# Spectral and token mixer on one core: the spectral path moved back by one pair, and VectorE and ScalarE held to the written order in the second product

## The chip, the core and the metric

One core of a Trainium2 chip runs the whole program in one launch. TensorE multiplies matrices into PSUM, VectorE and ScalarE do the elementwise work, GpSimd and SyncE issue most of the transfers. The metric is device time in microseconds (us), and lower is better. The kernel before took 385.02 us, the median of three runs (384.89 to 386.52).

## What is computed

The input `x` has 2048 tokens of 512 channels, all in float32. The reference is

```
xn = layernorm(x)
s  = irfft2( rfft2(xn) * (w_r + 1j*w_i) )            # over tokens and channels
h  = layernorm(xn)
u  = gelu( einsum("bsd,sf->bdf", h, w1) + b1 )       # F = 1792, along the tokens
y  = einsum("bdf,fs->bds", u, w2) + b2
out = x + s * silu(y transposed back)
```

The change lies in the last third of the kernel: the product with `w2`, the gate `silu(y)`, the last transforms of the spectral path (`s`), and `x + s * gate`.

## The kernel before, in words

**The second product.** The 2048 output tokens form 16 row blocks of 128 tokens (`NJ`), taken as eight pairs: block `p` and block `p + 8`. A pair is a 2 x 2 block product by Strassen's scheme in Winograd's form, so seven products of half size stand in place of eight. They run in the order `ORDER = (1, 2, 5, 6, 3, 7, 4)`, and this text calls them product 1, product 2, product 5 and so on. Each is 21 matmuls: seven blocks along F, and for each the three terms high x high, high x low and low x high of a split of float32 into two parts (`FORMS`, line 140 in the profile, since the helper that records TensorE's work has that line).

**PSUM in a pair.** Products 1, 6, 7 and 4 add up in bank `bx`, product 2 goes to `by`, and products 5 and 3 add up in `bz`. Between them the running sums are read out: `p1` copies `bx` after product 1, `p5` copies `bz` after product 5, `v2` copies `bx` after product 6 (`copied`, line 883, ScalarE). `summed` (line 891, VectorE) adds a bank and such a copy: `c11 = by + p1`, `c12 = bz + v2`, `c22 = bx + p5`. `gate` (line 887, ScalarE) is the Silu of that. So product 6 must not write `bx` before `p1` is read, nor product 3 write `bz` before `p5` is, nor product 7 `bx` before `v2`, nor product 4 before `c22`.

**Weights of a product ("forms").** Each product needs its own combination of blocks of `w2`, split in two: ScalarE writes the high part (line 749, here "high 5" for product 5), VectorE the low part (line 750, "low 5"). The forms lie in three buffers (`w2p`, tag `w2f`, `bufs=3`), so the form of a product can be written once the product three places before it has ended. Products 5, 6 and 3 take theirs from one tile, `s1`, that is changed in between: low 5, then `s1 += a12`, high 6, low 6, `s1 += a11`, high 3, low 3 (`added_up`, line 759, VectorE, "add"). The blocks come by DMA one pair ahead (line 736 on SyncE, and line 738 on GpSimd, which adds a second block on top of the first).

**The spectral path of a pair.** `gathered` (lines 831 to 836) collects the pair's frequencies in `yt`, with one small ScalarE copy and two VectorE operations for each block. `channels` (TensorE, into banks 6 and 7) is the inverse transform along the channels; the profile shows it as `ps<-cd,yt`. `unfolded` (lines 851 to 867) turns that into `y` in three pieces: a ScalarE copy with a sum and a difference; four sums; two scaled sums. `spectral` (`ps<-y,cft`, banks 0 and 1) is the last transform along the tokens. `finish` (lines 895 to 902) multiplies it by the gate and sends the block out, which GpSimd's transfer adds to `x` in the output; the last block adds `x` on VectorE.

**What sets the order.** The framework orders each engine's instructions by its own model, unless an instruction is kept in program order: then it stands behind all that was recorded for its engine before it. `Kept` wraps an engine so that each of its operations is kept. In the kernel before, TensorE is kept from the middle of the kernel on, VectorE and ScalarE are kept by `step` for the stretch ahead of the loop over pairs (`in_order`), and free in the loop itself. Each engine works off its instructions one after another.

**The start of the loop.** Ahead of it the last blocks of the hidden layer are made: `gelu`, and the parts of `u` in the combinations that the products read. `form_d` serves product 1, `form_a` products 2 and 3, `form_c` products 5 and 6, `form_b` products 7 and 4 (high part line 312, low part line 313, `sums` lines 338 to 341 between `form_a` and `form_c`). Block 6 of `u` is the last, and the last that each product reads. In the kernel before, the order at this place was: forms d, c and b of block 5, form of product 5, then a, sums, c, `s1 += a12` and b of block 6. `gathered(0)` came next, and `channels(0)` stood behind product 2 of pair 0. Later pairs have `spectral(p)` and `channels(p+1)` between products 7 and 4 of pair `p`.

Of the kernel before, what the change touches and what calls it, by code (L numbers as in the profile page):

```python
# [142 lines left out]
def spectral_mixer_kernel(tc, x, w1, b1, w2, b2, wk, we, wx, c_f, c_ft, c_d, c_i, c_g, c_h, c_t, out):  # L143
# [14 lines left out]
    with tc.tile_pool(name="ps", bufs=1, space=PSUM) as psp, ExitStack() as left, ExitStack() as right:  # L158
# [141 lines left out]
        def step(instruction):  # L300
            return keep(instruction) if in_order else instruction
# [439 lines left out]
        def s1_load(p, where):  # L741
            return w2_load("s1", where, p + NP, 0, (p + NP, 1))

        def w2_form(name, src):
# [4 lines left out]
            step(A.activation(parts[:, 0], v, AF.Copy))  # L749
            step(V.tensor_sub(parts[:, 1], v, parts[:, 0].bitcast(F32)))  # L750
            return wf

        nxt = {"a12": w2_load("a12", w2p, 0, 1, queue=G), "a11": w2_load("a11", w2p, 0, 0, queue=G)}
        in_order.append(True)
# [3 lines left out]
        def added_up(t, other):  # L758
            step(V.tensor_add(t, t, other))  # L759

        def w2_forms():

            for p in range(NP):
                yield w2_form(f"1_{p}", cur["a12"])
                yield w2_form(f"2_{p}", cur["a11"])
                yield w2_form(f"5_{p}", cur["s1"])
                if p:
                    added_up(cur["s1"], cur["a12"])
                w = w2_form(f"6_{p}", cur["s1"])
                if p + 1 < NP:  # L770
                    nxt["s1"] = s1_load(p + 1, (w2p, fp)[(p + 1) % 2])
                    nxt["a12"] = w2_load("a12", w2p, p + 1, 1)
                yield w
                added_up(cur["s1"], cur["a11"])
# [12 lines left out]
                yield w  # L787
# [18 lines left out]
        form_a(6)  # L806
        sums(6)
# [5 lines left out]
        lstage.close()  # L813
        fp = pool(left, "left", "fin", 1)
        cur["a21"] = w2_load("a21", fp, NP, 0)
        T = Kept(nc.tensor, keep)
        halved = (slice(0, 64), slice(0, None, 2)), (slice(64, P), slice(1, None, 2))
        xr = fp.tile([P, D], F32, name="xr")
        for rows, tokens in halved:
            SY.dma_start(xr[rows], x[tokens, NJ - 1])  # L820

        def gathered(p):

# [23 lines left out]
        def unfolded(p):  # L847

            pe = ps[:, 6:8].rearrange("p i (h k) -> p i h k", h=2)
            od = fp.tile([P, 2, 256], F32, name=f"od{p}", tag="od")  # L850
            A.activation(od, pe[:, :, 1], AF.Copy)
            es = fp.tile([P, 2, 2, 2, P], F32, name=f"es{p}", tag="es")
            V.tensor_add(es[:, :, 0].rearrange("p i b c -> p i (b c)"), pe[:, :, 0], od)  # L853
            V.tensor_sub(es[:, :, 1].rearrange("p i b c -> p i (b c)"), pe[:, :, 0], od)  # L854
            yield
            t = od.rearrange("p a b -> p (a b)")[:, :256].rearrange("p (i h c) -> p i h c", i=2, h=2)
            V.tensor_add(t[:, :, 0], es[:, :, 1, 1, :64], es[:, :, 1, 1, 64:])
            V.tensor_sub(t[:, :, 1], es[:, :, 1, 1, 64:], es[:, :, 1, 1, :64])
            y = fp.tile([P, 2, 2, 2, 2, 64], F32, name=f"y{p}", tag="y")
            ev = es[:, :, :, 0].rearrange("p i h (q c) -> p i h q c", c=64)  # L860
            ov = es[:, :, 0, 1].rearrange("p i (h c) -> p i h c", c=64)
            V.tensor_add(y[:, 0, :, :, 0], ev[:, :, :, 0], ov)  # L862
            V.tensor_sub(y[:, 1, :, :, 0], ev[:, :, :, 0], ov)  # L863
            yield
            ev = ev[:, :, :, 1].rearrange("p i h c -> p (i h) c")
            for s, sc in ((0, RT), (1, -RT)):
                V.scalar_tensor_tensor(y[:, s].rearrange("p i h q c -> p (i h) q c")[:, :, 1], t.rearrange("p i h c -> p (i h) c"), sc, ev, op0=ALU.mult,
                                       op1=ALU.add)
            ys[p] = y.rearrange("p s i h q c -> p s i (h q c)")
            yield  # L870
# [30 lines left out]
                else:  # L901
                    SY.dma_start(out[tokens, j, cols], g[rows, cols])

        left_, right_, whole = slice(0, HD), slice(HD, D), slice(0, D)
        yts, ys, pieces, gathering = {}, {}, iter(()), iter(())
        run(gathered(0))
        for p in range(NP):
            j0, j1 = p, p + NP
            more = p + 1 < NP
            g0, g1 = (fp.tile([P, D], F32, name=f"g{j}", tag="g", bufs=2) for j in (j0, j1))  # L910
            bx, by, bz = ps[:, 2 + p % 2, :HD], ps[:, 4, :HD], ps[:, 5, :HD]
            for k, n in enumerate(ORDER):
                wf = ready.pop(0)
                w = next(wforms, None) if p + k else None
                if w is not None:
                    ready.append(w)
                o = {1: bx, 6: bx, 7: bx, 4: bx, 2: by, 5: bz, 3: bz}[n]
                for m, i in enumerate(FORMS):
                    uh, ul = form_parts(n, i)
                    for a, (wi, ui) in enumerate(((0, uh), (0, ul), (1, uh))):  # L920
                        T.matmul(o, wf[:, wi, i], ui, start=m + a == 0 and n in (1, 2, 5), stop=m == NH - 1 and a == 2,
                                 skip_group_check=n in (6, 3, 7, 4))
                if n == 1:
                    p1 = copied(f"p1_{p}", bx)
                    if more and p:
                        gathering = gathered(p + 1)
                elif n == 5:
                    p5 = copied(f"p5_{p}", bz)
                    if more and not p:
                        gathering = gathered(p + 1)  # L930
                elif n == 2:
                    gate(g0, j0, left_, summed(f"c11_{p}", by, p1), 1.0)
                    if p == 0:
                        channels(p)
                        pieces = unfolded(p)
                elif n == 6:
                    v2 = copied(f"v2_{p}", bx)
                    if not more:
                        spectral(p)
                elif n == 3:  # L940
                    gate(g0, j0, right_, summed(f"c12_{p}", bz, v2), 1.0)
                    if not more:
                        finish(g0, j0, whole)
                elif n == 7:
                    gate(g1, j1, right_, summed(f"c22_{p}", bx, p5), -1.0)
                    if more:
                        spectral(p)
                        run(gathering)
                        channels(p + 1)
                        pieces = unfolded(p + 1)  # L950
                        finish(g0, j0, whole)
                    else:
                        finish(g1, j1, right_)
                else:
                    gate(g1, j1, left_, bx, -1.0)
                    finish(g1, j1, whole if more else left_)
                if n in (2, 5, 6, 3, 1, 4):
                    next(pieces, None)
                    if n != 4:
                        next(gathering, None)  # L960


# [35 lines left out]
```

## Time and profile before

| | |
|---|---|
| median of 3 runs | 385.02 us |
| profiled execution, its own time | 384.9 us |
| its span in the profile | 382.9 us |
| outside the span | 2.0 us |
| granted TensorE clock, mean | 0.993 |
| VectorE busy, 232.4 to 355.6 us (six pairs) | 101.0 of 123.2 us |
| ScalarE busy, the same stretch | 62.7 of 123.2 us |

A row of the timeline gives the start in us from the start of the span, the duration, the engine, the line, the operation with its tiles and shapes, and how many instructions were merged; brackets give the engine's idle time ahead of it and what ended it. `PE` is TensorE, `DVE` VectorE, `ACT` ScalarE. A row of the stretches gives, for a window of time, each engine's busy time with its instruction count, then the granted clock of TensorE, the DMA share and GB/s. TensorE's ends are modelled, so starts are used here, and a product is measured from its start to the next product's.

### The profile page before, as it was taken

Reading aid. Unit: us, or ns where it says so; the run is one execution under the profiler, and the core shown is the slowest. Engines: PE = TensorE matmul, PEld = TensorE weight load, DVE = VectorE, ACT = ScalarE, POOL = GpSimd, SP = SyncE. Lnnn points to the kernel's source line nnn. Section 1 sums busy time; section 2 is a strip of 40 time slices with the busy share of each in tenths; the row PEclk is TensorE's granted clock in tenths of the full one; section 3 lists DMA queues with packets and bytes.
Section 4 is the critical chain, followed back from the end, with each engine's and each line's share of the span. In section 5 each row is a group of like instructions: output and inputs, shape, how many; then the busy total and the mean of one; then the engine's idle time right before and its main releaser. Section 6 shows DMA issues by size and latency. Waiting matters only on the chain.

```text
span 382.9 us, 7730 instructions
## 1 busy us (share of the span) xinstructions
PE 370.4 (97%) x2888; PEld 321.1 (84%) x2888; DVE 322.4 (84%) x643; ACT 211.1 (55%) x382; POOL 86.2 (23%) x139
## 2 busy tenths in 40 slices
PE   8999999999999999999999599999999999999993
PEld 4888888888878777777888599999999989898993
DVE  6899999984689999999998989788787879796762
ACT  4676776762963444476547644645554553636341
POOL 1133223231222222221020014040313122140301
PEclk9999999999999999999999899999999999999998
DMA  7884776304375565866465598696969687885703
GB/s 238 289 283 165 261 256 243 98 1 125 103 237 205 184 229 183 265 199 215 142 242 96 171 225 156 184 195 161 201 154 239 127 234 139 230 148 160 104 0 55
DMA packets 34404, 68.35 MB, mean 178 GB/s; under 512 B 4656, under 2 KB 17856, under 8 KB 34240
## 3 DMA queue, kind: packets, MB, share of 16 engines
q1 hardware_dynamic: 25920, 43.09, 34.9%
q0 software_dynamic: 8448, 24.78, 29.2%
q8 instruction: 22, 0.36, 0.4%
q14 instruction: 14, 0.11, 0.1%
HBM read 59.47 MB, written 8.13 MB: 177 GB/s over the span
## 4 chain that ended last, share of the span: by engine, by line
PE 86%; DVE 9%; ACT 3%; issue 1%; POOL 0%; ACTq 0%; POOLq 0%
PE ps L140 61%; PE ps L408 20%; PE ps L247 4%; DVE w2f L750 3%; DVE s L759 2%; ACT w2f L749 2%; PE ps L397 1%; DVE yt L836 1%; DVE yt L835 1%; DVE g L895 1%; DVE es L854 0%; DVE es L853 0%; DVE c L891 0%; DVE y L862 0%; DVE y L863 0%
## 5 line engine op out<-in xcount | busy, mean ns | idle before, releaser
L408 PE MATMUL ps<-h,w1h 128*128 128x512 f32 x224 | 58.5, 398 | 0.0
L140 PE MATMUL ps<-h,w1h 128*128 128x512 f32 x176 | 56.2, 400 | 0.0
L408 PEld LDWEIGHTS ps<-h,w1h 128*128 128x128 f32 x224 | 40.9, 188 | 7.9
L750 DVE TENSOR_TENSOR w2f<-s,w2f 128x896 fp32r<-128x896 f32 x32 | 34.9, 1091 | 11.9 <-ACT w2f L749 11.0
L140 PE MATMUL ps<-fa,w2f 128*128 128x256 f32 x336 | 43.6, 281 | 1.1 <-DVE w2f L750 1.1
L140 PEld LDWEIGHTS ps<-fa,w2f 128*128 128x128 f32 x336 | 40.7, 188 | 3.0 <-DVE w2f L750 2.2
L140 PE MATMUL ps<-fb,w2f 128*128 128x256 f32 x336 | 42.5, 280 | 0.6 <-DVE c L891 0.6
L749 ACT ACTIVATE w2f<-s 128x896 fp32r<-128x896 f32 x32 | 32.8, 1026 | 15.5 <-DVE s L759 15.5
L140 PE MATMUL ps<-fc,w2f 128*128 128x256 f32 x336 | 41.2, 282 | 0.0
L140 PEld LDWEIGHTS ps<-fb,w2f 128*128 128x128 f32 x336 | 40.3, 188 | 0.8 <-issue 0.8
L140 PEld LDWEIGHTS ps<-h,w1h 128*128 128x128 f32 x176 | 31.6, 188 | 10.7 <-issue 4.9
L140 PEld LDWEIGHTS ps<-fc,w2f 128*128 128x128 f32 x336 | 40.4, 191 | 0.0
L738 POOL DMA_DIRECT2D s<-in_w_dram x16 | 14.0, 883 | 106.2 <-DMA s<-in_w_dram 60.1
L750 DVE TENSOR_TENSOR w2f<-a,w2f 128x896 fp32r<-128x896 f32 x24 | 26.1, 1092 | 11.3 <-ACT w2f L749 10.6
L140 PE MATMUL ps<-h,w1l 128*128 128x512 f32 x88 | 34.4, 391 | 0.0
L749 ACT ACTIVATE w2f<-a 128x896 fp32r<-128x896 f32 x24 | 24.8, 1038 | 16.8 <-PE ps L140 9.1
L900 POOL DMA_DIRECT2D out_dram<-g x30 | 25.2, 983 | 36.7 <-DVE g L895 30.7
L408 PE MATMUL ps<-h,w1l 128*128 128x512 f32 x112 | 30.6, 389 | 0.0
L408 PEld LDWEIGHTS ps<-h,w1l 128*128 128x128 f32 x112 | 21.0, 188 | 4.5
L591 POOL DMA_DIRECT2D xc<-xc x16 | 9.8, 620 | 64.1 <-ACT xc L588 46.6
L140 PEld LDWEIGHTS ps<-cd,yt 128*128 128x128 f32 x128 | 15.7, 200 | 10.1 <-issue 5.7
L403 DVE TENSOR_TENSOR w1l<-w1r,w1h 128x512 fp32r<-128x512 f32 (+1 forms) x32 | 20.9, 652 | 2.1 <-ACT w1h L400 1.9
(114 smaller groups left out, 700.4 us busy)
## 6 DMA issues: line engine op xcount, KB each, us to landing
a<-in_w_dram SPq DMA_DIRECT2D x22, 448.0 KB, 4.0
wt<-in_wk_dram POOLq DMA_DIRECT2D x16, 512.0 KB, 5.3
s<-in_w_dram SPq DMA_DIRECT2D x16, 448.0 KB, 4.2
s<-in_w_dram POOLq DMA_DIRECT2D x16, 448.0 KB, 6.3
w1s<-in_w_dram SPq DMA_DIRECT2D x36, 128.0 KB, 2.6
w1r<-in_w_dram SPq DMA_DIRECT2D x16, 256.0 KB, 3.1
xc<-xc POOLq DMA_DIRECT2D x16, 256.0 KB, 3.0
x<-in_x_dram SPq DMA_DIRECT2D x15, 256.0 KB, 3.8
```

The source lines that it names most:

```text
L140: return lambda *args, **kw: self.keep(operation(*args, **kw))
L247: T.matmul(z[:, b], h[:, b * P:(b + 1) * P], c, start=True, stop=True)
L397: T.matmul(ps[:, 0], wz[:, :P], wz, start=True, stop=True)
L403: keep(V.tensor_sub(dst, src, hi.bitcast(F32)))
L408: T.matmul(ps[:, bank + i], w[wi][:, i * P:(i + 1) * P], hj, start=first and j == 0, stop=last and j == NJ - 1)
L591: keep(G.dma_start(*(v.rearrange("p s t c -> p s (t c)") for v in (there[c::2], here[1 - c::2, ::-1]))))
L738: G.dma_start(t, w2_half(*added), accum_op=ALU.add)
L749: step(A.activation(parts[:, 0], v, AF.Copy))
L750: step(V.tensor_sub(parts[:, 1], v, parts[:, 0].bitcast(F32)))
L759: step(V.tensor_add(t, t, other))
L835: yield V.tensor_add((same, other)[i], first, second)
L900: G.dma_start(out[tokens, j, cols], g[rows, cols], accum_op=ALU.add)
```

## The change

Four things change, all in the second product. (1) `V` and `A` become `Kept` in the loop, so VectorE and ScalarE follow the written order there. (2) In the loop, the next form is taken behind the product, not ahead of it, and so it stands ahead of that product's copy, sum and gate; behind product `k` comes the form for the product three places later, as the buffers allow. (3) `spectral(p-1)`, `channels(p)` and `finish(p-1)` stand behind product 7 of pair `p` (behind product 6 in the last pair), and a table, `SLOTS`, says behind which products the steps of `gathered` ("g") and the pieces of `unfolded` ("s") run. The gates get four buffers for two, since they wait a pair longer. (4) Ahead of the loop, `form_b` of blocks 5 and 6 comes last, product 1 of pair 0 is recorded earlier, and `s1 += a12` and the high part of product 6's form stand ahead of `sums(6)`. Beside these, `od` goes (its place is taken by the second half of `es`, and by a part of `y`), and `xr` lies in a buffer of `s1` and is loaded in the last pair.

```diff
+SLOTS = ((5, {3: "gggg", 5: "s"}), (5, {2: "gg", 3: "s", 4: "ggs", 5: "s"}), (3, {0: "s", 1: "sgggg", 3: "s", 4: "ss"}))
...
-                yield w2_form(f"5_{p}", cur["s1"])
-                if p:
-                    added_up(cur["s1"], cur["a12"])
-                w = w2_form(f"6_{p}", cur["s1"])
+                w = w2_form(f"5_{p}", cur["s1"])
+                added_up(cur["s1"], cur["a12"])
+                yield w
+                w = w2_high(f"6_{p}", cur["s1"])
+                if p == 0:
+                    yield
+                w = w2_low(*w)
+                added_up(cur["s1"], cur["a11"])
+                yield w
...
         form_c(5)
-        form_b(5)
         ready.append(next(wforms))
         gelu(6, 7)
         form_a(6)
+        products(0, ORDER[0])
+        next(wforms)
         sums(6)
         form_c(6)
-        added_up(cur["s1"], cur["a12"])
+        ready.append(next(wforms))
+        form_b(5)
         form_b(6)
+        lstage.close()
         in_order.clear()
-        V, A, T = nc.vector, nc.scalar, nc.tensor
+        V, A = Kept(nc.vector, keep), Kept(nc.scalar, keep)
...
         for p in range(NP):
+            slot, plan = SLOTS[min(p, 1) + (p + 1 == NP)]
+            gathering = gathered(p)
             for k, n in enumerate(ORDER):
+                if p + k:
+                    products(p, n)
+                    if n == 7:
+                        c22 = summed(f"c22_{p}", bx, p5)
+                    ready.extend(w for w in [next(wforms, None)] if w is not None)
+                if k == slot:
+                    if p:
+                        spectral(p - 1)
+                    channels(p)
+                    pieces = unfolded(p)
                 if n == 1:
                     p1 = copied(f"p1_{p}", bx)
+                elif n == 2:
+                    gate(g0, j0, left_, summed(f"c11_{p}", by, p1), 1.0)
                 elif n == 5:
                     p5 = copied(f"p5_{p}", bz)
...
+                if k == slot and p:
+                    for g, j in zip(gates.pop(p - 1), (j0 - 1, j1 - 1)):
+                        finish(g, j, whole)
+                for what in plan.get(k, ""):
+                    next(gathering if what == "g" else pieces)
...
+                if not more and k == 5:
+                    spectral(p)
+                    finish(g0, j0, whole)
+                    finish(g1, j1, right_)
+        finish(g1, j1, left_)
```

More of the change, by code (lines that the diff above doesn't have):

```diff
@@ L902, in finish @@
                     SY.dma_start(out[tokens, j, cols], g[rows, cols])
-        left_, right_, whole = slice(0, HD), slice(HD, D), slice(0, D)
-        yts, ys, pieces, gathering = {}, {}, iter(()), iter(())
-        run(gathered(0))
+        yts, ys, gates, pieces = {}, {}, {}, iter(())
         for p in range(NP):
@@ L936, in spectral_mixer_kernel @@
                 elif n == 6:
                     v2 = copied(f"v2_{p}", bx)
-                    if not more:
-                        spectral(p)
                 elif n == 3:
                     gate(g0, j0, right_, summed(f"c12_{p}", bz, v2), 1.0)
-                    if not more:
-                        finish(g0, j0, whole)
                 elif n == 7:
[L945 to L953, printed above, removed]
+                    gate(g1, j1, right_, c22, -1.0)
@@ L954, in spectral_mixer_kernel @@
                 else:
                     gate(g1, j1, left_, bx, -1.0)
[L956 to L960, printed above, removed]
+                if k == slot and p:
[3 more added lines that the diff above has]
+                    next(gathering if what == "g" else pieces)
@@ L964 @@
+                if not more and k == 2:
+                    xr = fp.tile([P, NH * P], F32, name="xr", tag="s1", bufs=1)[:, :D]
+                    for rows, tokens in halved:
+                        SY.dma_start(xr[rows], x[tokens, NJ - 1])
+                if not more and k == 5:
[3 more added lines that the diff above has]
+        finish(g1, j1, left_)
 def kernel(**inputs):
```

70 lines of the change are left out of this document (32 added, 38 removed).

## The prediction, made before the kernel ran

> **What bounds the kernel now.** First the page's first part, then two windows: TensorE's clock around its one long wait, and six whole pairs.
>
> ```profile
> PE 370.4 (97%) x2888; PEld 321.1 (84%) x2888; DVE 322.4 (84%) x643; ACT 211.1 (55%) x382; POOL 86.2 (23%) x139
> ```
>
> ```profile
> 216.90:220.40 3.50, 3.50 (x20) 3.50 (x19) 3.15 (x6) 2.17 (x6) 0.00 (x0) 0.52 1.05 340
> ```
>
> ```profile
> 232.40:355.60 123.20, 122.14 (x1028) 115.36 (x1027) 100.96 (x157) 62.74 (x102) 29.84 (x35) 1.00 0.77 177
> ```
>
> TensorE is busy 97% of the span, so a change of order can win little, and only where it waits. Six pairs take 123.20 us, 20.53 each. The timeline of TensorE shows the start of the loop, and further below one steady pair:
>
> ```profile
> 206.79 2.64 PE L140 MATMUL ps<-fd,w2f 128*128 128x256 f32 x21
> 209.27 2.63 PE L140 MATMUL ps<-fa,w2f 128*128 128x256 f32 x21
> 216.09 2.94 PE L140 MATMUL ps<-cd,yt 128*128 128x128 f32 x16 [4.19 <-DVE yt L836]
> 218.68 6.00 PE L140 MATMUL ps<-fc,w2f 128*128 128x256 f32 x42
> 224.52 2.63 PE L140 MATMUL ps<-fa,w2f 128*128 128x256 f32 x21
> ```
>
> ```profile
> 239.89 5.11 PE L140 MATMUL ps<-fc,w2f 128*128 128x256 f32 x42
> 244.84 2.90 PE L140 MATMUL ps<-fa,w2f 128*128 128x256 f32 x21
> 247.57 2.63 PE L140 MATMUL ps<-fb,w2f 128*128 128x256 f32 x21
> 250.13 1.09 PE L140 MATMUL ps<-y,cft 64*64 64x512 f32 x8
> 251.16 2.05 PE L140 MATMUL ps<-cd,yt 128*128 128x128 f32 x16
> 252.96 2.72 PE L140 MATMUL ps<-fb,w2f 128*128 128x256 f32 x21
> ```
>
> Start to start, products 5 and 6 take 4.95, so a product is 2.47; `spectral` is 1.03 and `channels` 1.80. A pair without waits is 7 x 2.47 + 1.03 + 1.80 = 20.12. The steady pair loses 0.4, mostly in product 3 (2.73 for 2.47), which waits for its low form. The big loss is at the start: from product 2 (209.27) to product 3 (224.52) there are three products and `channels`, 9.21 without waits, and 15.25 were taken: 6.0 us lost, 4.19 as a wait for `yt`, the rest because the clock stood at half for 3.5 us (0.52 above).
>
> **Prices of the hand-overs.** ScalarE and VectorE in the same steady pair:
>
> ```profile
> 242.00 0.51 ACT L887 ACTIVATE g<-c,b2t 128x256 f32<-128x256 f32 x1 [1.54 <-DVE c L891]
> 243.02 1.02 ACT L749 ACTIVATE w2f<-s 128x896 fp32r<-128x896 f32 x1 [0.52 <-DVE s L759]
> 243.95 0.37 ACT L883 ACTIVATE p<-ps 128x256 f32<-128x256 f32 x1
> 244.22 1.03 ACT L749 ACTIVATE w2f<-s 128x896 fp32r<-128x896 f32 x1
> 245.13 0.39 ACT L883 ACTIVATE v<-ps 128x256 f32<-128x256 f32 x1
> 245.39 1.05 ACT L749 ACTIVATE w2f<-a 128x896 fp32r<-128x896 f32 x1
> 247.77 1.03 ACT L749 ACTIVATE w2f<-a 128x896 fp32r<-128x896 f32 x1 [1.33 <-PE ps L140]
> ```
>
> ```profile
> 240.48 1.09 DVE L750 TENSOR_TENSOR w2f<-s,w2f 128x896 fp32r<-128x896 f32 x1 [0.30 <-ACT w2f L749]
> 241.49 0.42 DVE L891 TENSOR_TENSOR c<-ps,p 128x256 f32<-128x256 f32 x1
> 241.83 1.08 DVE L759 TENSOR_TENSOR s<-s,a 128x896 f32<-128x896 f32 x1
> 244.08 2.29 DVE L750 TENSOR_TENSOR w2f<-s,w2f 128x896 fp32r<-128x896 f32 x2 [1.17 <-ACT w2f L749]
> ```
>
> ```profile
> 233.11 0.64 DVE L836 TENSOR_TENSOR yt<-ey 128x240 f32<-128x240 f32 x1
> 233.57 0.70 DVE L853 TENSOR_TENSOR es<-ps,od 128x512 f32<-128x512 f32 x1
> ...
> 235.21 0.29 DVE L857 TENSOR_TENSOR od<-es 128x128 f32<-128x128 f32 x1
> 235.42 0.28 DVE L858 TENSOR_TENSOR od<-es 128x128 f32<-128x128 f32 x1
> 235.61 0.42 DVE L862 TENSOR_TENSOR y<-es 128x256 f32<-128x256 f32 x1
> ```
>
> Start to start where nothing waits: low 1.01 (240.48 to 241.49), a sum of 256 0.34, a high 0.93, a copy 0.27, a `yt` operation 0.45, the two small sums 0.21 each. Hand-overs: end of a product to ScalarE 0.20 (247.57 to 247.77), high to low 0.04 (244.04 to 244.08), add to high 0.11 (242.91 to 243.02), sum to gate 0.09 (241.91 to 242.00). To TensorE I allow 0.05, an estimate of the size of the others. So low follows 1.06 behind the start of its high, a high 1.19 behind the start of an add, a gate 0.51 behind the start of its sum. One more thing is to be seen: product 5 ended at about 242.4 (half of 4.95 after 239.89), yet its copy `p5` ran at 243.95, behind a high that had waited 0.52 for an add. Whatever stands behind a waiting instruction on ScalarE waits too.
>
> **The change in a steady pair.** No work goes away, apart from nothing measurable: highs, lows, sums and products are as many as before, and the new places of `od` (writing a part of `y` or of `es`) change no shape; between nothing and the 0.29 of such an operation I take nothing. What moves is the order. Let t = 0 be the start of product 1. High 5 now needs the buffer of product 4, which ended at 0. Then, each in the written order:
>
> - high 5 at 0.20, low 5 1.26, add 2.27, high 6 3.46, low 6 4.52, add 5.53, high 3 6.72, low 3 7.78. Before, low 3 stood at 9.1 (244.08, with product 1 two products ahead of 239.89), and it is what product 3 waited for: that wait is cured.
> - `c11` now stands behind low 3: 8.79. The gate of `c11`: 9.30. Behind this gate stand high 7 (9.72) and only then `p5` (10.65 to 11.02), although product 5 ended at 7.41. Queued behind the gate are the copy and, through it, TensorE: product 3 adds into the bank that `p5` reads. It could start at 4 x 2.47 = 9.88 and starts at 11.07. **A new wait of 1.19.**
> - VectorE, idle from 9.13 on, waits for high 7 too: low 7 at 10.78. Behind it, in the written order, stand two `yt` operations (11.79), low 4 (12.69), four sums of piece two (13.70: 0.21, 0.21, 0.34, 0.34), low 1 of the next pair (14.80, its high released by product 3 at 13.54 + 0.20), `c12` (15.81), two `yt` (16.15), and the two scaled sums of piece three (17.05, 17.39, done 17.81). `spectral(p-1)` needs these, and product 7 ends at 11.07 + 4.94 = 16.01. **A second new wait of 1.85**, to 17.86.
> - Then `spectral` to 18.89, `channels` to 20.69 (`yt` has been done since 17.2), product 4 to 23.16. `c22`, two `finish` products and piece one lie beside these.
>
> Nothing carries over: VectorE and ScalarE are idle again when product 4 ends, so the cycle closes at **23.16 us a pair against 20.53**. Six such pairs cost 15.8 us more. VectorE's work, 101.0 / 6 = 16.8 a pair, would fit in 20.1; it comes too late, since 4 to 5 us pass idle in the first eleven while the chain of `s1` goes back and forth. The gain of 0.4 in product 3 is in these numbers.
>
> **The change at the start.** ScalarE there, before:
>
> ```profile
> 206.77 0.61 ACT L312 ACTIVATE fb<-u 128x512 fp32r<-128x512 f32 x1
> 207.29 1.01 ACT L749 ACTIVATE w2f<-s 128x896 fp32r<-128x896 f32 x1
> 208.21 0.68 ACT L307 ACTIVATE u<-ps,b1t 128x512 f32<-128x512 f32 x1
> 208.92 0.63 ACT L312 ACTIVATE fa<-u 128x512 fp32r<-128x512 f32 x1
> 211.69 0.63 ACT L312 ACTIVATE fc<-u 128x512 fp32r<-128x512 f32 x1 [2.14 <-DVE u L340]
> ...
> 215.70 1.28 ACT L887 ACT_TABLE_LOAD   x1
> ```
>
> Without b of block 5, high 5 comes 0.52 earlier, at 206.77; low 5 207.83, add 208.84, low a of block 6 209.85. Before, that ran right behind its high part, at 209.59; so all that follows is 0.26 later: high c at 211.95, low c at 212.62. Product 5 starts at 209.27 + 2.47 = 211.74 without waiting, since block 6 is its last (needed at 213.9). Low 6 at 213.23 to 214.32 meets product 6, which starts at 214.21 and reads it third. **The wait of 4.19 and the half clock are gone.** But add runs at 214.24, high 3 at 215.43, low 3 behind the two late b parts (2 x 0.61) at 216.49, `c11` 217.50, gate 218.01 (the table load, 1.28 behind high 3, is over), high 7 218.43, `p5` 219.36 to 219.73. Product 3 starts at 219.78, not at 216.68: **3.10 waited in the new place.** Product 7 ends at 224.72, `channels` at 226.52, product 4 at 228.99. High 4 needs `a21`, whose transfer now waits for the late b of block 5 (done 215.9):
>
> ```profile
> a<-in_w_dram SPq DMA_DIRECT2D x22, 448.0 KB, 4.0
> ```
>
> By 4.0 us it has landed at about 220, when ScalarE is free for it, so it costs nothing; if it lands later by more than 1 us, product 7 waits for `v2` behind it, by as much. The other loads of a pair have ten us and more. The 30 output transfers of `finish` come a pair later, from GpSimd, which is 23% busy.
>
> **The last pair.** It starts at 228.99 + 6 x 23.16 = 367.95. Up to `p5` it is the same. `spectral(6)` runs behind product 6, and `channels(7)` waits for four `yt` operations (9.81 to 11.80) and ends at 13.65; products 3 and 7 end at 18.59, when `y` is done too (18.51), `spectral(7)` at 19.62, product 4 at 22.09. `c22` lies beside `spectral(7)`. What follows is as before: from the gate's start to the end of the span
>
> ```profile
> 377.58 0.47 ACT L887 ACTIVATE g<-ps,b2t 128x256 f32<-128x256 f32 x1 [2.35 <-PE ps L140]
> ```
>
> 382.9 - 377.58 = 5.32, and 0.20 ahead of it. Sum: 367.95 + 22.09 + 5.52 = 395.6 of span. With the 2.0 outside the span that is 397.6, against 384.9 for the profiled execution: 12.7 more, or **397.7 beside the median of 385.02**, 3.3% slower.
>
> **Rivals.**
>
> 1. *Faster.* My chain hangs on one point: that high 5 is released only by the end of product 4. If its buffer came free with product 7, `channels`, `spectral` and product 4 (5.3 us) would lie beside the chain; from 3.04 us earlier on (1.19 + 1.85) both new waits are gone. Then product 2 at 209.27, five products, `channels` and product 4 put pair 1 at 225.89, six pairs take 6 x 20.12, the last 21.15 and 5.52: 373.3, and 375.3 us. For it: VectorE has 16.8 of work in 20.1, ScalarE 10.5. Against it: three buffers, and the last row of ScalarE above, a high at 247.77 released by TensorE. The same would come if the written order weren't kept, but `Kept` covers every operation. Chance 0.08.
> 2. *Half of it.* Only `p5` holds TensorE, and the pieces are done in time. Then a pair takes 21.31, and the sum is 384.5 + 2.0 = 386.5, within 0.5% of before. It needs VectorE to run 1.85 us less between low 7 and the scaled sums, against 7.0 of rows shown. Chance 0.08.
> 3. *The clock falls.* The wait of 4.19 brought 3.5 us of half clock. If 3.10 does as well, product 3 and what follows lose 1.7: 399.4, still the forecast's case. If the two waits of each pair bring it, up to 1.7 of the 5.3 us of TensorE's work behind `spectral` are lost in each: 6 x 1.7, some 408. Chance 0.06.
>    The Trainium skill ("TensorE: Matmul & The Clock Gate", Part 1: The HAM clock gate) says that the clock is halved after at least one idle window of about 3.4 us, and that the windows run freely. By that rule the 4.19 could halve it, and the trace agrees, but 3.10 holds no whole window, and the sum stays 397.7; no wait of TensorE in the second product lies between 0.6 and 4.19 here, so no row tells.
>
> **How the numbers follow.** Forecast 0.75, the rivals 0.08, 0.08, 0.06, other slower outcomes (late transfers) 0.03. About 14 hand-overs lie on a pair's cycle: with none of their 0.04 to 0.20 the pair is 0.9 shorter, six pairs 5.5: 392; with 0.06 more each, 0.8 longer: 403, and the one clock drop of 1.7 lies inside. I take 390 to 403. Measurement tells about 0.5% (1.9 us) from no change. Faster: rival 1 and a little for a release that I misread, 0.10; same: rival 2, less its spread, 0.06; slower: the rest, 0.84.
>
> **What would show it.** Right: in each pair, TensorE waits twice, about 1.2 ahead of product 3 on `p5` (line 883) and about 1.9 ahead of `spectral` on the scaled sums; pairs of 23.2; ScalarE waits for `c11` ahead of a gate, and high 7 follows that gate; no wait for `yt` at the start. Wrong: pairs near 20.1, `p5` ahead of 9.9 after product 1, or the scaled sums done before product 7 ends.

## The result, and the profile after

The changed kernel took 415.68 us, the median of four runs (415.05 to 417.32), against 385.62 us for the kernel before (384.89 to 386.52): a ratio of 1.0785, with a 95% interval of 1.0743 to 1.0827. The prediction, 397.7 us, had the direction and fell 18 us short.

First the page's row of busy times and its row of TensorE's granted clock, of the kernel after:

```profile
PE 378.2 (91%) x2888; PEld 326.9 (79%) x2888; DVE 323.1 (78%) x643; ACT 209.9 (51%) x382; POOL 86.2 (21%) x139
```

```profile
PEclk9999999999999999999998998999989799999998
```

The count of matmuls is the same, and TensorE's share fell from 97% to 91%: the change put waits on TensorE, not work. The clock row has several dips now in its second half, in the loop; before it had one there, at the wait for `yt`, beside the last slice, which is lower in both. The waits of TensorE, by what it waited for (total us, times, longest):

```profile
PE ps L143 <- DVE y L143: 16.4, 8, 2.6
PE ps L143 <- ACT p L143: 11.8, 7, 4.3
```

These are the two waits that were forecast: `spectral` waits for the scaled sums of VectorE (`y`), product 3 for the copy `p5` of ScalarE (`p`). They are longer than forecast. The timeline of TensorE in one pair of the kernel after:

```profile
360.76 2.63 PE L143 MATMUL ps<-fd,w2f 128*128 128x256 f32 x21
...
372.01 2.74 PE L143 MATMUL ps<-fa,w2f 128*128 128x256 f32 x21 [1.20 <-ACT p L143]
374.59 2.63 PE L143 MATMUL ps<-fb,w2f 128*128 128x256 f32 x21
379.82 1.09 PE L143 MATMUL ps<-y,cft 64*64 64x512 f32 x8 [2.60 <-DVE y L143]
380.84 2.05 PE L143 MATMUL ps<-cd,yt 128*128 128x128 f32 x16
382.64 2.72 PE L143 MATMUL ps<-fb,w2f 128*128 128x256 f32 x21
385.20 2.63 PE L143 MATMUL ps<-fd,w2f 128*128 128x256 f32 x21
```

The pair takes 385.20 - 360.76 = 24.44. Product 3 starts 11.25 behind product 1 (11.07 forecast), `spectral` 19.06 behind it (17.86). Not every pair is as short. The stretches of three of the six pairs, and a window inside the first (the granted clock stands behind the five engines):

```profile
232.50:258.56 26.06, 22.25 (x173) 20.75 (x172) 17.01 (x26) 10.38 (x17) 5.11 (x6) 0.93 0.67 150
258.56:282.93 24.37, 20.56 (x173) 19.34 (x172) 16.92 (x26) 10.41 (x17) 4.87 (x6) 1.00 0.64 146
...
308.98:336.30 27.32, 23.53 (x173) 21.51 (x172) 17.00 (x26) 10.36 (x17) 5.12 (x6) 0.88 0.65 140
...
252.10:255.40 3.30, 3.30 (x20) 2.52 (x13) 2.05 (x3) 0.30 (x1) 1.42 (x3) 0.52 0.68 136
```

Three of the six pairs (the third of them, left out here, takes 26.05) are 1.6, 1.6 and 2.9 us longer than the other three (24.37 to 24.46), and in these the clock was at half for some us behind the wait ahead of `spectral`.

The start of the loop in the kernel after, TensorE from product 3 of pair 0 on, and then ScalarE:

```profile
221.78 4.16 PE L143 MATMUL ps<-fa,w2f 128*128 128x256 f32 x21 [4.25 <-ACT p L143]
225.77 2.63 PE L143 MATMUL ps<-fb,w2f 128*128 128x256 f32 x21
```

```profile
218.75 1.28 ACT L143 ACT_TABLE_LOAD   x1 [1.54 <-DVE c L143]
220.05 0.51 ACT L143 ACTIVATE g<-c,b2t 128x256 f32<-128x256 f32 x1
```

The wait for `yt` is gone, as forecast. Product 3 waits 4.25 in its place (3.10 forecast), and then runs for 225.77 - 221.78 = 3.99 at half clock. The load of the Silu table (`ACT_TABLE_LOAD`) stands inside the chain here: it starts only when `c11` is there.

The stretches of pair 0, of pairs 1 to 6 and of the last pair up to its product 4, in the kernel before and in the kernel after:

```profile
206.79:234.94 28.15, 23.96 (x188) 22.80 (x187) 25.17 (x44) 15.34 (x28) 4.26 (x5) 0.94 0.68 175
234.94:358.20 123.26, 122.20 (x1029) 115.42 (x1028) 100.35 (x156) 62.49 (x100) 29.85 (x35) 1.00 0.77 176
358.20:374.84 16.64, 16.03 (x137) 14.92 (x135) 11.35 (x17) 7.45 (x12) 2.63 (x4) 1.00 0.22 29
```

```profile
207.33:232.50 25.17, 20.92 (x164) 20.63 (x163) 18.92 (x28) 13.97 (x23) 2.59 (x3) 0.93 0.63 173
232.50:385.20 152.70, 129.54 (x1028) 121.15 (x1027) 101.68 (x156) 62.27 (x102) 29.69 (x35) 0.96 0.64 142
385.20:405.09 19.89, 19.12 (x160) 17.09 (x159) 16.41 (x30) 8.52 (x15) 3.55 (x5) 1.00 0.33 51
```

The end of the kernel after, the last gate, the last adding transfer of GpSimd, and the drain of GpSimd's queue:

```profile
407.78 0.47 ACT L143 ACTIVATE g<-ps,b2t 128x256 f32<-128x256 f32 x1 [2.88 <-PE ps L143]
```

```profile
406.27 1.67 POOL L933 DMA_DIRECT2D out_dram<-g  x2 [2.47 <-DVE g L143]
```

```profile
L1018 POOLq DRAIN  x3: 46/93/7874, 406.7 to 415.1; - x3
```

From the gate's start to the end of the span it is 415.3 - 407.78 = 7.52, where before it was 5.32. Cut at these points, the spans compare so:

| stage (us) | before | forecast | after |
|---|---|---|---|
| up to product 1 of pair 0 | 206.79 | 206.79 | 207.33 |
| pair 0, to product 1 of pair 1 | 28.15 | 22.20 | 25.17 |
| pairs 1 to 6 | 123.26 | 138.96 | 152.70 |
| last pair, to product 4 | 16.64 | 19.62 | 19.89 |
| from there to the end | 8.06 | 7.99 | 10.21 |
| span | 382.9 | 395.6 | 415.3 |

So 13.7 of the 19.7 us that the forecast missed in this execution (417.32 us, the longest of the four) lie in the six pairs, 3.0 in pair 0, 2.2 at the very end.

### The profile page after: what moved, and what is told of

Same layout as the page of the kernel before. It is cut to its first block, busy times and chain, and to the rows that moved or that the text cites. A ratio compares the mean times of both kernels' runs of the same rounds, so it can differ in the third digit from the quotient of the medians.

```text
span 415.3 us, 7713 instructions
## 1 busy us (share of the span) xinstructions
PE 378.2 (91%) x2888; PEld 326.9 (79%) x2888; DVE 323.1 (78%) x643; ACT 209.9 (51%) x382; POOL 86.2 (21%) x139
## 5 line engine op out<-in xcount | busy, mean ns | idle before, releaser
L143 DVE TENSOR_TENSOR w2f<-s,w2f 128x896 fp32r<-128x896 f32 x30 | 32.8, 1093 | 37.8 <-ACT w2f L143 37.7
L143 ACT ACTIVATE w2f<-s 128x896 fp32r<-128x896 f32 x30 | 30.4, 1012 | 44.2 <-DVE s L143 28.6
L143 PEld LDWEIGHTS ps<-fa,w2f 128*128 128x128 f32 x336 | 42.0, 194 | 13.2 <-ACT p L143 13.2
L143 PE MATMUL ps<-fb,w2f 128*128 128x256 f32 x336 | 43.4, 284 | 0.0
L143 PEld LDWEIGHTS ps<-fb,w2f 128*128 128x128 f32 x336 | 41.3, 191 | 0.8 <-DVE c L143 0.8
L143 ACT ACTIVATE g<-c,b2t 128x256 f32<-128x256 f32 x24 | 12.2, 508 | 32.9 <-DVE c L143 32.9
L143 ACT ACTIVATE w2f<-a 128x896 fp32r<-128x896 f32 x22 | 22.6, 1028 | 12.1 <-issue 12.1
L143 DVE TENSOR_TENSOR w2f<-a,w2f 128x896 fp32r<-128x896 f32 x22 | 23.9, 1088 | 3.4 <-ACT w2f L143 2.5
L143 PE MATMUL ps<-y,cft 64*64 64x512 f32 x64 | 9.9, 690 | 16.4 <-DVE y L143 16.4
L143 PEld LDWEIGHTS ps<-cd,yt 128*128 128x128 f32 x128 | 19.1, 236 | 6.8 <-issue 5.9
```

The lines of the kernel that those rows point to most:

```text
L143: return lambda *args, **kw: self.keep(operation(*args, **kw))
```

## The experiments

The theory was that of the prediction: the written order puts two waits on one chain of VectorE and ScalarE. The rivals were that holding the two engines to any order costs this much, and that the falling clock, not the chain, is the cost. Times are medians, beside 384.92 to 385.74 for the kernel before on the same chips; the ratio is to the kernel before. Differences to the changed kernel are those of the medians, 415.68 less the run's. Runs 1, 3, 5, 6 and 8 came within the range that was expected of them; the others are said to miss it where they do.

**1. The order set free.** Everything else of the change stays.

```diff
-        V, A = Kept(nc.vector, keep), Kept(nc.scalar, keep)
+        V, A = nc.vector, nc.scalar
```

> The changed kernel, but VectorE and ScalarE are not kept in the written order in the loop over pairs; the start of the loop, the places of spectral and channels, and the recorded order stay. Theory (written order: the copy p5 behind the gate of c11, the pieces behind four forms, and the clock that falls in these waits): without it a ready copy or piece can go first, so a pair falls from 24.4 us to 20.2 to 21.5, no half clock in the pairs, 386 to 396 us in all. Rival (the later place of the spectral path itself, or its transfers, makes the wait): the wait ahead of spectral stays near 2.6, above 405 us.

Measured: 389.53, ratio 1.0122 (1.0092 to 1.0151). The waits of TensorE in the loop, and the stretch of one pair:

```profile
PE ps L143 <- ACT p L916: 6.8, 7, 3.5
```

```profile
252.79:273.85 21.06, 20.59 (x174) 19.44 (x173) 16.57 (x28) 10.49 (x17) 5.14 (x8) 1.00 0.78 180
```

The pair is 21.06, and no wait for `y` is in the list: `spectral` finds its sums ready. What is left is a wait for a copy, 3.5 in pair 0 and 0.4 to 0.8 in the others. So 26 of the 30 us lost are in the order of VectorE and ScalarE in the loop, and not in the later spectral path, whose place on TensorE is the same here. That doesn't yet say whether it is this order or any order.

**2. The copy, sum and gate ahead of the next form.** The next form is taken behind them.

```diff
                 if p + k:
                     products(p, n)
-                    ready.extend(w for w in [next(wforms, None)] if w is not None)
...
                     gate(g1, j1, left_, bx, -1.0)
+                if p + k:
+                    ready.extend(w for w in [next(wforms, None)] if w is not None)
```

> The changed kernel with each next form taken behind the copy, sum and gate of its product, not ahead of them. Theory A (the two waits of a pair sit on one chain): the wait of 1.2 us ahead of product 3 falls to about 0.2, but high 1 then stands behind the gate of c12, so the scaled sums come about 19.1 us after product 1, the wait ahead of spectral grows from 2.6 to about 4 us, a pair stays at 24.4 to 24.6, and longer waits bring the half clock in more pairs: 414 to 424 us. Rival B (the two waits are separate prices that add up): 6 x 1.2 and the clock's share are saved, about 405 us.

**3. The pieces and the `yt` operations earlier.** Piece two runs behind product 4 and piece three behind product 1 of the next pair (before, behind products 6 and 3), and the `yt` operations behind products 2 and 5 (before, 5 and 3).

```diff
-SLOTS = ((5, {3: "gggg", 5: "s"}), (5, {2: "gg", 3: "s", 4: "ggs", 5: "s"}), (3, {0: "s", 1: "sgggg", 3: "s", 4: "ss"}))
+SLOTS = ((5, {3: "gggg", 5: "s", 6: "s"}), (5, {0: "s", 1: "gg", 2: "gg", 5: "s", 6: "s"}), (3, {0: "s", 1: "gggg", 3: "s", 4: "ss"}))
```

> The changed kernel with the table of places changed alone: piece two of unfolded behind product 4, piece three behind product 1, where VectorE waits for the chain of s1, and the steps of gathered behind products 2 and 5. Theory: the wait ahead of spectral (2.6 us) is gone, that ahead of product 3 stays at 1.2 to 1.6, a pair takes about 21.8, and with no wait over 2 us no half clock in the pairs: 391 to 397 us. Rival (the low forms or the chain of s1 bound the pair, not the pieces): a pair stays above 23.5, above 405 us.

**4. Both moves together.**

> Both edits at once: each next form behind its product's copy, sum and gate, and the pieces early. If the two waits sit on one chain whose VectorE part is cut by the early pieces, moving the forms now helps, where alone it did not: the wait ahead of product 3 falls from 1.4 to 1.7 us to about 0.9 (the low form of product 3 behind the gate of c11), no wait ahead of spectral, a pair about 21.1, 386 to 391 us. If the order of copies and forms is worth nothing by itself (as it was alone): 396 us again, as with the early pieces only.

Measured: move 2 alone 424.76 (1.1037, 1.0943 to 1.1131), slower by 9.1 than the changed kernel; move 3 alone 396.19 (1.0295, 1.0265 to 1.0325), 19.5 faster; both 391.65 (1.0153, 1.0101 to 1.0206), 24.0 faster and 0.65 above the range expected. Move 2 alone is 0.76 above its range. A move that costs 9.1 alone gains 4.5 once the other is there. TensorE in a pair with move 2 alone:

```profile
275.65 1.99 PE L143 MATMUL ps<-y,cft 64*64 64x512 f32 x8 [3.72 <-DVE y L143]
```

and with move 3 alone, with the pair's stretch:

```profile
266.70 2.74 PE L143 MATMUL ps<-fa,w2f 128*128 128x256 f32 x21 [1.73 <-ACT p L143]
```

```profile
255.29:277.14 21.85, 20.12 (x174) 18.98 (x173) 17.12 (x26) 10.28 (x17) 5.16 (x9) 1.00 0.75 172
```

With the copy ahead of the form, product 3 of that pair waits for nothing, so product 7 ends earlier, by 1.3; the pieces that `spectral` needs are hardly earlier (it starts 18.85 behind product 1, for 19.06), and most of the gain turns up as wait there: 3.72 for 2.60. And behind this longer wait `spectral` itself takes 1.99 for 1.09, at half clock. That is where most of the 9.1 come from: all six pairs have the half clock now and take 25.66 to 27.25, where 24.4 to 24.6 were expected and half clock in more of them; the granted clock over the span fell from 0.976 to 0.944. With the pieces out of the chain, the wait ahead of `spectral` is gone and the pair 21.85. This is what a chain does that ends in two places: whoever cures the first wait only sees the second grow.

**5. The waits of TensorE filled.** Matmuls whose result nobody reads run in the waits, so that TensorE isn't idle: 33 ahead of product 3 of pair 0, then 9 ahead of each product 3 and 20 ahead of each `spectral`. Nothing that the program needs comes earlier by that.

```diff
+                if n == 3 and more:
+                    idle(p, 9 if p else 33)
                 if p + k:
                     products(p, n)
...
                 if k == slot:
+                    if p and more:
+                        idle(p, 20)
                     if p:
                         spectral(p - 1)
```

> The changed kernel with extra matmuls of 128x256 that nothing reads, into the unused half of an idle bank: 33 ahead of product 3 of pair 0, 9 ahead of product 3 and 20 ahead of spectral in pairs 1 to 6, sized to end within the waits. Theory (the waits let the clock fall to half, and that lies on the path): no half clock in the pairs, a pair 24.4 everywhere, about 7 us less: 406 to 411 us. Rival (the half clock lies beside the waits and costs nothing): 414 to 417 us.

Measured: 410.71 (1.0672, 1.0641 to 1.0703), 5.0 faster than the changed kernel, where about 7 were expected, by work that is of no use. Nearly all of the six pairs in one stretch:

```profile
232.00:378.00 146.00, 142.32 (x1189) 134.98 (x1188) 101.57 (x156) 62.21 (x102) 29.20 (x35) 1.00 0.68 150
```

The clock is 1.00, where the six pairs of the kernel after have 0.96. The half clock is thus 5.0 of the 18 us by the medians (1.5 to 7.2 by the ends of the two intervals), and it is a consequence of the waits, not a rival to them: with the clock at full speed the kernel is still 26 us slower than before.

**6. The Silu table loaded early.** One column goes through Silu behind `p1` of pair 0, so that the table is there before the gate.

```diff
                     p1 = copied(f"p1_{p}", bx)
+                    if p == 0:
+                        A.activation(fp.tile([P, 1], F32, name="early"), b2t[:, :1], AF.Silu)
```

> The changed kernel with one Silu of a single column behind the copy p1 of pair 0, so that ScalarE's table for Silu is loaded while it waits for the sum of s1, and not ahead of the first gate. Theory (the table load of 1.28 us stood in the chain to p5 of pair 0, where the prediction had it hidden): the wait ahead of product 3 of pair 0 falls from 4.25 to about 3.0 us, 1.3 to 3 us less in all depending on the clock: 411 to 415 us. Rival (the load waits for something else, or another step bounds that place): the wait stays above 4 us.

Measured: 414.33 (1.0741, 1.0687 to 1.0796), 1.35 faster. The intervals overlap, so the time alone doesn't tell; the trace does. The wait in pair 0 fell from 4.25 by 1.27, about the length of the table load:

```profile
219.84 4.21 PE L143 MATMUL ps<-fa,w2f 128*128 128x256 f32 x21 [2.98 <-ACT p L143]
```

The clock fell to half behind the shorter wait all the same: the product takes 4.21.

**7. Both copies of `gathered` in its first step.** The second block's small ScalarE copy no longer stands behind the gate of `c12`.

```diff
             for i, j in enumerate((p, p + NP)):
-                t = yt[:, i]
...
                 A.activation(to, ey[:, :, 0:4, j].rearrange("p b (e s) c -> p b e s c", e=2), AF.Copy)
+            for i, j in enumerate((p, p + NP)):
+                t = yt[:, i]
```

> The changed kernel with both small ScalarE copies of gathered in its first step, so that the second pair of yt operations no longer waits for a copy that stands behind the gate of c12. Theory (this wait of 0.7 us of VectorE, which the prediction lacked, lies on the chain to spectral): the wait ahead of spectral falls from 2.6 to about 1.9, a pair without half clock from 24.4 to 23.7, some 4 us less in all: 410 to 413 us. Rival (the copy is beside the chain): 415 to 417 us, and the wait stays at 2.6.

Measured: 409.61 (1.062, 1.0583 to 1.0657), 6.1 faster, 0.4 under the range expected. A pair at full clock, `spectral` and the whole stretch:

```profile
275.85 1.09 PE L143 MATMUL ps<-y,cft 64*64 64x512 f32 x8 [1.82 <-DVE y L143]
```

```profile
257.57:281.23 23.66, 20.65 (x173) 19.43 (x172) 16.82 (x26) 10.37 (x17) 4.95 (x6) 1.00 0.66 150
```

The wait ahead of `spectral` is 1.82, which is the 1.85 of the forecast, and the pair 23.66. Six times 0.78 is 4.7; the rest of the 6.1 is half clock that didn't come: two pairs have it in this trace, 1.65 each, where three had it.

**8. The prices that the forecast had missed, taken away together.** Moves 6 and 7, the filled waits (23, 9 and 14 matmuls), and the last pair's first block sent out by SyncE, with `x` added on VectorE, for GpSimd's adding transfer.

> The changed kernel with the four things that the prediction had priced at nothing taken out at once: the table load early, both copies of gathered early, the waits of TensorE filled (23 extra matmuls ahead of product 3 of pair 0, 9 ahead of product 3 and 14 ahead of spectral in pairs 1 to 6), and block 7 out by SyncE. Theory (these are the misses, and they add up): 415.7 - 1.3 - 5.0 - 4.2 - 2.4 = 402.8, so 401 to 405 us, against the 397.7 that was forecast; what is left over is the hand-overs, and pairs take 23.7. Rival (they cover each other, or another miss is as large): above 406 us.

Measured: 402.32 (1.0431, 1.0396 to 1.0465), as expected.

**9. The chain taken apart.** Moves 2, 3 and 6 (the `yt` operations behind products 5 and 6, not 2 and 5), with the step's `yt` operations and pieces ahead of the next form, and product 5 and `p5` of pair 0 ahead of the form of product 3 and of the gate. All operations stay in the written order. The start of pair 0, as the core of the edit:

```diff
+                    if p + k == 1 and not p:
+                        products(0, 5)
+                        p5 = copied("p5_0", bz)
+                        ready.append(next(wforms))
```

> The written order kept on VectorE and ScalarE, and the order itself mended: copy, sum and gate first, then the pieces, then the next form; piece two behind product 4, piece three behind product 1, the steps of gathered behind products 5 and 6; in pair 0 the table load early and product 5 with its copy ahead of the form of product 3. Theory: a pair without waits over 0.4 us, about 20.3; pair 0 waits about 0.8 ahead of product 3, no half clock in the loop: 378 to 382 us, faster than the kernel before by 1 to 2%. Rival (a kept order costs something of its own that the free order does not): above 385 us.

**10. The same, and the last pair's first block out by SyncE.**

```diff
-            if j + 1 == NJ:
-                V.tensor_add(g[:, cols], g[:, cols], xr[:, cols])
+            if j in xl:
+                V.tensor_add(g[:, cols], g[:, cols], xl[j][:, cols])
```

> As the repaired kernel, and in the last pair block 7 also gets its x on VectorE and leaves by SyncE, not by GpSimd's adding transfer. Theory (the end of the span waits for GpSimd, whose last transfer is issued about 1.5 us before the last gate in the changed order, where it was 3.7 us before the last gate in the kernel before, and the span from the start of the last product grew from 8.1 to 10.2 us): about 2 us less than the repaired kernel, 376 to 380 us. Rival (the tail is set by SyncE's last transfer): the same time as the repaired kernel within 0.5 us.

**11. The same as 10, and the gate of `c11` behind `p5` in every pair, with two steps of `gathered` of pair 0 moved forward.**

> As the repaired kernel with block 7 by SyncE, and two more moves: the gate of c11 behind the copy p5, so that high 3 doesn't stand behind it, and in pair 0 two steps of gathered behind product 5, so that c22 comes earlier. Theory (what is left of the waits is low 3 behind the gate of c11, 0.35 in a pair of 20.6, and c22 in pair 0, 1.84): pairs of 20.2 to 20.4 and about 3.5 us less than the repaired kernel with its tail: 379 to 382 us. Rival (the pair of 20.6 is TensorE's own pace, and the 0.35 only shows where it is faster): pairs stay at 20.5 to 20.6, and only pair 0 gains, 381.5 to 384 us.

Measured: 386.09 (1.0007, 0.9986 to 1.0028), 383.66 (0.9956, 0.9933 to 0.998) and 383.65 (0.9944, 0.9923 to 0.9966). All three are 1.6 to 4.1 us above the range that the theory gave them, and run 9 lies in that of its rival (above 385: a held order costs something of its own). Its pairs speak against that rival: the six take 20.58 each on average, in run 10 20.59, and 20.54 in the kernel before. So the held order costs next to nothing in the pairs once it is a good one, which settles the first rival. The last two are faster than the kernel before by 0.4 and 0.6%, little, but their intervals lie below 1. The rival's range held in run 11, where five of the six pairs have no wait on TensorE left that the trace shows. One of them

```profile
250.10:270.64 20.54, 20.54 (x173) 19.43 (x172) 16.91 (x27) 10.33 (x17) 5.15 (x8) 1.00 0.79 183
```

```profile
262.46 2.86 PE L143 MATMUL ps<-fb,w2f 128*128 128x256 f32 x21
265.26 1.09 PE L143 MATMUL ps<-y,cft 64*64 64x512 f32 x8
```

takes 20.54, where the kernel before takes 20.53. Its product 7, 2.80 from start to start, is 0.33 longer than 2.47, so something is still late by that; but in the kernel before, a pair with a wait of 0.35 ran its products faster, at 2.38:

```profile
275.96 2.54 PE L140 MATMUL ps<-fd,w2f 128*128 128x256 f32 x21
278.34 2.54 PE L140 MATMUL ps<-fa,w2f 128*128 128x256 f32 x21
```

So the 0.4 that the prediction counted as a loss of the steady pair was not to be had by any order tried here. That TensorE holds a pace of about 20.5 a pair is the reading; it was argued, not shown. What these versions win is the start of the loop, less new waits there of 0.62 to 1.84.

## Why the prediction fell short, point by point

The mechanism was right, and the direction with it. What failed are terms of the sum that were put at nothing or too small: the small ScalarE copy of `gathered`, which was left out of the chain to `spectral`; the clock, which had a chance of 0.06 and no price; the table load; the end; and some short steps.

- **The two waits, their places and their causes: right.** Product 3 waits on `p5` behind high 7 and the gate, 1.20 for 1.19. `spectral` waits on the scaled sums. Runs 2 to 4 showed that both hang on one chain.
- **"`c12` (15.81), two `yt` (16.15)": the step that failed in each pair.** VectorE was followed in its own order, but the second block's two `yt` operations need a small ScalarE copy, and this stands behind the gate of `c12`. VectorE, from `c12` on, and ScalarE from the same gate on, in the kernel after:

```profile
376.90 0.42 DVE L143 TENSOR_TENSOR c<-ps,v 128x256 f32<-128x256 f32 x1
378.01 1.04 DVE L143 TENSOR_TENSOR yt<-ey 128x240 f32<-128x240 f32 x2 [0.69 <-ACT yt L143]
378.89 0.87 DVE L143 SCALAR_TENSOR_TENSOR y<-y,es 128x256 f32<-128x256 f32 x2
```

```profile
377.35 0.51 ACT L143 ACTIVATE g<-c,b2t 128x256 f32<-128x256 f32 x1 [1.49 <-DVE c L143]
377.77 0.21 ACT L143 ACTIVATE yt<-ey 128x32 f32<-128x32 f32 x1
```

  Sum, gate, copy and then `yt`: 378.01 - 376.90 = 1.11 for the 0.34 counted. That is 0.77 a pair, 4.6 in six, and run 7 gave 0.78 a pair back.
- **The short steps: sized a little short.** The rest of the pair, 24.44 - 23.16 - 0.77 = 0.51, is 3.0 in six. It is spread: 0.18 up to product 3 (11.25 for 11.07), 0.24 on VectorE behind that, and 0.09 in the product behind `channels` (385.20 - 382.64 = 2.56 for 2.47). Little of it is hand-overs. The first part is in the low forms and adds of `s1`, in the kernel after:

```profile
362.05 1.09 DVE L143 TENSOR_TENSOR w2f<-s,w2f 128x896 fp32r<-128x896 f32 x1 [1.52 <-ACT w2f L143]
363.17 1.09 DVE L143 TENSOR_TENSOR s<-s,a 128x896 f32<-128x896 f32 x1
```

  An add, which changes what the low form has just read, starts 1.12 behind it, here and in the other place of the pair 1.13; the forecast took the 1.01 of a low form with a sum of other tiles behind it. Twice that is 0.23, and shorter steps behind give some back. Product 3 takes 374.59 - 372.01 = 2.58 for 2.47, which makes low 1 later, and the two scaled sums 0.87 for 0.76. `spectral` starts 0.06 behind its sums (378.89 + 0.87 = 379.76), as allowed. The 0.8 that the range allowed for hand-overs would cover this term alone, not the others.
- **"The sum stays 397.7": the clock fell, and rival 3 came true in part.** Run 5 puts the half clock at 5.0 us. The prediction gave it a chance of 0.06 and thought only of the 3.10 in pair 0, and of up to 1.7 a pair; three pairs of six lost 1.6, 1.6 and 2.9.
  The Trainium skill ("TensorE: Matmul & The Clock Gate", Part 1: The HAM clock gate) says that at least one idle window of about 3.4 us halves the clock, and that windows run freely. The traces disagree with the first: a wait of 2.60 halved it in three of six pairs, and 2.98 in run 6. That the same wait halves it in one pair and not in the next agrees with free windows, and the forecast that leaned on the whole window was wrong.
- **"The table load, 1.28 behind high 3, is over": wrong.** In the kernel before, the load began right behind the copy `p1` (215.70), and the gate behind it still waited for `c11`:

```profile
217.76 0.51 ACT L887 ACTIVATE g<-c,b2t 128x256 f32<-128x256 f32 x1 [0.78 <-DVE c L891]
```

  In the kernel after, it is the load that waits, 1.54, and it starts at the moment when `c11` is there, so it is on the chain: 1.3 us, which run 6 took out of the wait. It needn't be so: in run 2, where the gate stands behind `p1` without a form between, the load again starts right behind the copy, and only the gate waits:

```profile
213.91 1.28 ACT L143 ACT_TABLE_LOAD   x1
217.00 0.51 ACT L143 ACTIVATE g<-c,b2t 128x256 f32<-128x256 f32 x1 [1.81 <-DVE c L143]
```

- **"What follows is as before": wrong by 2.2.** The rows of the end show a drain of GpSimd's queue (the row gives the shortest, middle and longest of three in ns, and the first and last start) of 7.87 us, which begins 0.4 behind the start of its last adding transfer and ends at 406.7 + 7.87 = 414.6; the span ends at 415.3. In the kernel before, the row of that transfer and of the drain are

```profile
373.88 1.66 POOL L900 DMA_DIRECT2D out_dram<-g  x2 [12.28 <-DVE g L895]
```

```profile
L994 POOLq DRAIN  x3: 46/102/7864, 374.3 to 382.7; - x3
```

  The transfer began 0.96 ahead of the last product (374.84), and the drain ended at 374.3 + 7.86 = 382.2, also 0.7 ahead of the end of the span. `finish` of the last pair comes later now, and the transfer begins 1.18 behind the last product's start. "From GpSimd, which is 23% busy" looked at the queue's load and not at when it comes to an end. Run 10 differs from run 9 by this alone and is 2.4 faster. Its drain begins at 367.1 and ends at 367.1 + 8.90 = 376.0, 4.4 ahead of the end of its span of 380.4:

```profile
L1026 POOLq DRAIN  x3: 46/102/8899, 367.1 to 380.1; - x3
```

The terms, beside the forecast of 397.7: half clock 5.0, the ScalarE copy 4.6, the short steps 3.0, the end 2.2 to 2.4, the table load 1.3; 16.1 to 16.3 of 18.0. Product 1 of pair 0 also starts 0.5 later after than before, but it starts anywhere from 206.59 to 207.54 in the runs, which are the same up to there, so this is scatter and no price of the change. Run 8, with four of the terms taken away, came to 402.3; the short steps are in it still, 3.0, and 1.6 is left that no run assigned. Run 5 may put the half clock too low, by up to 1.0: its pairs take 24.59 on average, where those of the kernel after without half clock take 24.42.

In the profiled execution, where 19.7 were missed, the rows of the trace leave next to nothing over: half clock 6.2 in the pairs and 1.5 in product 3 of pair 0, the ScalarE copy 4.6, the short steps 3.0, product 3 of pair 0 later by 1.5 (14.45 behind product 1, for 12.99; the table load is 1.3 of it), the end 2.2, the last pair 0.3, and the late start 0.5.

The gain that was to be had at the start was used up there: pair 0 is 3.0 shorter than before, but 2.8 of that, a `spectral` and a `channels`, only went to the last pair. The new wait of 4.25 with its half clock took what the cured one gave. In run 10, where pair 0's waits are 0.62, 0.24 and 1.84, pair 0 takes 22.65, and there the gain is to be seen.

## What to carry to other kernels

When two engines in program order hand a value back and forth, follow every operand of every instruction on both, however small: a copy of 0.21 us behind a gate cost 0.77 in each pair. A wait that is cured on a chain with two ends turns up at the second; move the end that is out of the cycle first, here the pieces. And price a wait on TensorE with the clock that it may lose, and a late adding transfer of GpSimd with its drain at the end of the program.

## What the runs showed of the hardware that was not expected

- The clock fell to half behind waits much shorter than the 4.19 of the kernel before: 2.60 in three of six pairs. With waits of 1.82 (run 7), beside those of 1.20 to 1.55 ahead of product 3, it still did so in two of six, so the 2 us that were expected to be safe in run 3 are no limit. With one wait of 1.36 to 1.74 a pair (run 3) it did so in none of the six pairs. Where it is decided, and what picks the pair, wasn't settled.
- A table load can wait with the instruction behind it, although the table could have been loaded during the wait: 1.54 idle ahead of the load in the kernel after and in runs 3, 5 and 7. In the kernel before and in runs 2 and 4 it didn't, and the gate alone waited (0.78, 1.81 and 1.81). What decides it wasn't settled.
- The queue of GpSimd took 7.86 us (before) and 7.87 us (after, and run 9) to drain, from 0.4 us behind the start of its last adding transfer, and 8.90 us in run 10, where its last four transfers stand together.
